# Last block of an S4 convolution: the spectrum's second turn of slots 4 to 7 in two parts, the low half's turn two slots earlier, two sums on GpSimd, one addition on VectorE

## The chip, the cores and the metric

The kernel runs on one core of a Trainium2 chip. The metric is the time of the whole program on the device in microseconds (us); one execution was also taken with the hardware profiler. TensorE (PE in the profile) multiplies matrices, VectorE (DVE), ScalarE (ACT) and GpSimd (POOL) do elementwise work, and SyncE (SP), ScalarE and GpSimd issue DMA transfers from queues of their own. Each engine works through its instructions in program order.

## The reference, cut to what matters

```python
def reference(A_u, A_A_re, ..., B_w1, B_b1, B_w2, B_b2):
    def _A_ref(u, ...):                     # diagonal state space convolution, length L = 2048
        P = jnp.exp(logdA[:, :, None] * l[None, None, :])
        K = jnp.einsum("dn,dnl,dn->dl", Cc, P, dB).real
        Kf, Uf = rfft(pad(K)), rfft(pad(u))
        return irfft(Uf * Kf)[..., :L] + u * Dskip
    def _B_ref(x, w1, b1, w2, b2):
        return gelu(x @ w1 + b1) @ w2 + b2
    x = A_u                                 # (1, 2048, 512)
    xn = _layernorm(x)
    s = _A_ref(xn, ...)
    g = silu(_B_ref(xn, ...))
    return x + s * g
```

Only the convolution `s`, its product with the gate `g` and the addition of `x` bear on the change.

## The kernel before, in words

The first 390 us or so compute the layer norm, the feed-forward gate `g` and the convolution kernels, by a long order written out by hand. The convolution follows, in four blocks of 128 channels (`b` = 0 to 3), each in eight slots (`g` = 0 to 7, function `slot`). The transform of length 4096 is factored into parts of 32 and 64 points. The order of the instructions on every engine is that of the code.

In a slot of the last block TensorE makes the second part of the forward transform of four frequencies (`second_tiles`, L891, tile `s`, in PSUM with two buffers `ri`); ScalarE copies the signal's half (`uh`), VectorE multiplies it with the kernel's spectrum (L910, or L924 in slot 7, two products), and sums and differences of the products give the real and imaginary spectrum `Y` (`combine`, L934 and L936; on GpSimd for slots 0 and 1, else on VectorE). Every two slots make one `Y`; TensorE transforms it back over 64 points (`back_dft`, L945, tiles `sa_p` and `sa_q`), ScalarE copies the result into `Z` (`back_out` L955, `last_out` L963), and VectorE turns `Z` in 32x32 blocks into `T`. `Z` and `T` have a low half, from slots 0 to 3 (turned by `turn`, L989), and a high half, from slots 4 to 7 (turned by `last_turn`, L969).

Slot 7 is done in two columns `jj` with a PSUM tile of their own each (`last_second`, `last_product`), the first of which takes the buffer of slot 5 and the second that of slot 6. Their two columns of `Y` feed the back transform into `sa_q`.

Behind the slots stands the end of the program. `last_half(b, h, i)` is the last transform, over 32 points, of half `h` of the spectrum into output half `i` (L982, `y`): 16 matmuls with 32x32 weights out of `gc` and 256 columns; the results of both `h` add up in PSUM. The profile has two rows for a matmul of float32. An output half has two quarters of the output, `n[0]` and `n[1]`, or `n[2]` and `n[3]`. VectorE multiplies them with the gate: `last_gate_low` (L1040, two products a quarter) for `n[0]` and `n[1]`, `last_gate_high` (L1046, four products) for the rest. `last_add` (L1050) adds `x`: on GpSimd for `n[0]` and `n[1]`, on VectorE for `n[2]` and `n[3]`. `store` issues four transfers a quarter (L1055), on SyncE's and ScalarE's queues in turns, and two of `n[2]` on GpSimd's. The transfers of SyncE and ScalarE go over eight lanes, each with a semaphore; a store that takes a lane waits until the lane's transfer before it has landed.

The low half is turned in two pieces: one in slot 5, `turn(b, 0, 0)`, the other at the end of slot 7, `turn(b, 0, 1)`.

## Time before, and the profile's summary

| | |
|---|---|
| median of 3 runs | 528.2 us (527.54 to 529.6) |
| the profiled execution | 526.64 us |
| its span, first to last instruction | 524.9 us |
| TensorE busy | 507.3 us, 97% of the span |
| VectorE busy | 456.0 us, 87% |
| GpSimd busy | 326.6 us, 62% |
| granted TensorE clock, mean | 0.995 of full speed |

The span is what the rows of the trace cover; the execution's own time is 1.74 us longer. Rows are of one execution. Matmuls overlap, so a busy TensorE is not one at its peak; the last 8 us of the span, behind TensorE's last transforms, belong to the other engines.

### The profile page before, as it was taken

The page shows a single profiled execution, that of the slowest core. Times are in us where ns is not written, and L with a number is a line of the kernel's source. Part 1 is how long each engine was busy: PE and PEld are TensorE (multiplying, and loading weights), DVE is VectorE, ACT ScalarE, POOL GpSimd, SP SyncE. Part 2 cuts the span into 40 slices and gives each one's busy share as a digit, 9 for nine tenths or more (in the row PEclk, how much of TensorE's full clock was granted, in tenths as well). Part 3 has the DMA queues.
Part 4 walks back from the last instruction along what each step waited for, and adds up shares of the span by engine and source line. Part 5 has one row for each costly group of instructions (what it writes and reads, how often), then busy time and mean ns, then how long its engine had stood idle before and what let it go on. Part 6 is the DMA issues. An engine that isn't in the chain of part 4 may idle for free.

```text
span 524.9 us, 13548 instructions
## 1 busy us (share of the span) xinstructions
PE 507.3 (97%) x5439; PEld 372.3 (71%) x5439; DVE 456.0 (87%) x702; ACT 355.8 (68%) x514; POOL 326.6 (62%) x424
## 2 busy tenths in 40 slices
PE   7999999999999999999999999999999999999993
PEld 6777777777777777777777777777844565656671
DVE  6999989997889989999999898799766868597895
ACT  3749976898698789967979997987814333324340
POOL 5647798474848397975874746675236433947632
PEclk9999999999999999999999999999999999999997
DMA  7858875239275939050158467148496969365595
GB/s 202 213 158 232 256 230 161 68 99 307 61 197 168 286 105 338 15 201 31 32 172 214 127 186 196 35 84 165 115 358 220 177 145 144 99 142 101 123 231 132
DMA packets 108527, 85.63 MB, mean 163 GB/s; under 512 B 43436, under 2 KB 84400, under 8 KB 108464
## 3 DMA queue, kind: packets, MB, share of 16 engines
q1 hardware_dynamic: 98208, 65.81, 49.2%
q0 software_dynamic: 8928, 17.96, 11.6%
q10 hardware_dynamic: 1328, 0.98, 0.8%
q8 instruction: 43, 0.70, 0.6%
q14 instruction: 20, 0.16, 0.1%
HBM read 51.18 MB, written 33.55 MB: 161 GB/s over the span
## 4 chain that ended last, share of the span: by engine, by line
PE 66%; DVE 19%; ACT 5%; POOL 3%; issue 3%; POOLq 0%; DVEq 0%; ACTq 0%
PE s L891 10%; PE z L290 7%; PE z L291 7%; PE z L292 7%; PE f L251 6%; PE f L253 6%; PE f L252 6%; PE sa_p L945 6%; PE kg L664 4%; PE s L875 3%; PE ph L602 2%; DVE hl L277 2%; POOL mm L625 2%; DVE e L652 1%; DVE x L354 1%
## 5 line engine op out<-in xcount | busy, mean ns | idle before, releaser
L625 POOL TENSOR_TENSOR mm<-mm,rc 128x32 f32<-128x32 f32 (+4 forms) x150 | 110.0, 734 | 11.8
L290 PE MATMUL z<-w2h,hh 128*128 128x512 f32 x224 | 97.6, 436 | 0.0
L251 PE MATMUL f<-xh,w1h 128*128 128x512 f32 x220 | 90.5, 412 | 0.2 <-DVE xl L386 0.2
L292 PE MATMUL z<-w2h,hl 128*128 128x512 f32 x224 | 88.5, 395 | 0.6 <-DVE hl L277 0.6
L291 PE MATMUL z<-w2l,hh 128*128 128x512 f32 x224 | 88.6, 396 | 0.0
L253 PE MATMUL f<-xh,w1l 128*128 128x512 f32 x220 | 87.0, 395 | 0.0
L252 PE MATMUL f<-xl,w1h 128*128 128x512 f32 x220 | 86.8, 395 | 0.0
L891 PE MATMUL s<-X,mc 128*64 128x256 f32 x512 | 64.4, 393 | 0.6 <-issue 0.5
L910 DVE TENSOR_TENSOR t<-s,uh 128x512 f32<-128x512 f32 x62 | 39.6, 669 | 21.8 <-ACT uh L902 21.6
L622 POOL COPY mm<-rc 128x32 f32<-128x32 f32 x30 | 16.8, 560 | 64.4 <-DVE e L655 42.5
L891 PEld LDWEIGHTS s<-X,mc 128*64 128x64 f32 x512 | 34.2, 135 | 32.0 <-issue 7.6
L648 DVE TENSOR_TENSOR e<-mm,ra 128x1024 f32<-128x1024 f32 x32 | 43.3, 1354 | 14.2 <-ACT ra L636 8.6
L290 PEld LDWEIGHTS z<-w2h,hh 128*128 128x128 f32 x224 | 42.5, 190 | 12.6 <-issue 3.9
L265 ACT ACTIVATE hf<-f,b1s 128x512 f32<-128x512 f32 x56 | 38.1, 687 | 19.3 <-PE f L253 10.1
L902 ACT COPY uh<-s 128x512 f32<-128x512 f32 x31 | 18.2, 586 | 48.3 <-PE s L891 37.5
L292 PEld LDWEIGHTS z<-w2h,hl 128*128 128x128 f32 x224 | 42.1, 188 | 11.0 <-DVE hl L277 1.0
L277 DVE TENSOR_TENSOR hl<-hf,hh 128x512 fp32r<-128x512 f32 x56 | 47.9, 862 | 2.1 <-ACT hh L271 2.0
L253 PEld LDWEIGHTS f<-xh,w1l 128*128 128x128 f32 x220 | 41.3, 188 | 10.2 <-DVE w1l L236 0.3
L251 PEld LDWEIGHTS f<-xh,w1h 128*128 128x128 f32 x220 | 41.5, 189 | 9.9 <-DVE xl L386 0.5
L291 PEld LDWEIGHTS z<-w2l,hh 128*128 128x128 f32 x224 | 42.3, 189 | 8.4
L252 PEld LDWEIGHTS f<-xl,w1h 128*128 128x128 f32 x220 | 41.4, 188 | 9.3
L271 ACT CAST hh<-hf 128x512 fp32r<-128x512 f32 x56 | 34.5, 618 | 19.5 <-PE z L291 19.3
(194 smaller groups left out, 1092.5 us busy)
## 6 DMA issues: line engine op xcount, KB each, us to landing
xs<-x SPq DMA_DIRECT2D x16, 256.0 KB
xt_h<-xh POOLq DMA_DIRECT2D x4, 1024.0 KB, 5.9
xt_l<-xl POOLq DMA_DIRECT2D x4, 1024.0 KB, 7.8
kgd<-ko SPq DMA_DIRECT2D x16, 256.0 KB
za<-zo SPq DMA_DIRECT2D x4, 1024.0 KB
xh<-xt_h POOLq DMA_DIRECT2D x4, 1024.0 KB, 6.6
xl<-xt_l POOLq DMA_DIRECT2D x4, 1024.0 KB, 9.2
zi<-za SPq DMA_DIRECT2D x4, 1024.0 KB
```

The lines of the kernel that those rows point to most:

```text
L251: PE.matmul(p, wh[:, k, :], xh[:, k, :], start=(k == 0), stop=False)
L252: PE.matmul(p, wh[:, k, :], xl[:, k, :], start=False, stop=False)
L253: PE.matmul(p, wl[:, k, :], xh[:, k, :], start=False, stop=(k == KD - 1))
L265: A.activation(hf, pt.pop((v, f)), AF.Gelu_apprx_tanh, bias=b1s[:, f:f + 1])
L277: V.tensor_sub(hl, hf, hh)
L290: PE.matmul(z, hh[:, s], wh, start=(f0 == 0 and not rows), stop=False)
L291: PE.matmul(z, hh[:, s], wl, start=False, stop=False)
L292: PE.matmul(z, hl[:, s], wh, start=False, stop=(f0 == FA - 1))
L625: GP.tensor_mul(mv[:, :, 0:3:2, w:2 * w], mv[:, :, 0:3:2, 0:w], rc[:, 2 + 2 * i:4 + 2 * i, :].rearrange("p j c -> p c j").unsqueeze(3).to_ ...
L648: V.tensor_mul(e1, m1.unsqueeze(1).to_broadcast([P, 2, CH, N1]), ra[:, :, :, :N1])
L891: PE.matmul(p[ka * 64:(ka + 1) * 64, o], SB["mc"][:, 2 * k + jj, o, :], xf[b][:, k, :, :, jj], start=True, stop=True, skip_group_check=True)
L910: V.tensor_mul(sm[b, g // 2][i][:, :, 2 * (g % 2):2 * (g % 2) + 2], p[:, :, i, 1].unsqueeze(1).to_broadcast([P, 2, 2, P]), uh)
```

## The change

The high half's `Z` and `T` get a new shape: slots 4 and 5 (`j` = 0) and slots 6 and 7 (`j` = 1) have blocks of their own. A 32x32 block now holds two time steps, two parts (real, imaginary) and eight frequencies, where it held one step, two parts and sixteen. `last_turn(b, j, ia)` turns `j` = 0 in one instruction of 1024 elements and `j` = 1 in two of 512. The matmuls behind it, `last_quarter(b, j, i)`, read blocks that mix two steps, so `gc` gets four more sets of 32x32 weights, in which the rows of the other step are zero: 32 matmuls of 128 columns for each `j` and `i`, in place of 16 of 256 for both `j`. `gc` grows from 64 to 192 floats a partition (32 KB to 96 KB).

The other piece of the low half's turn goes from slot 7 to slot 5. The two sums of slot 7's first column go to GpSimd. The addition of `n[0]` goes from GpSimd to VectorE. The order of the last matmuls changes with the parts.

```diff
--- before.py
+++ after.py
@@ -129,7 +129,11 @@
     a = 2 * np.pi * n1 * (k1 + 0.25) / N1
     cf = np.tile(np.stack([np.cos(a), -np.sin(a)], 1), (G, 1, 1))
     cg = np.stack([np.cos(a).T, -np.sin(a).T]).reshape(2, 2, N1 // 2, N1)
-    cg = np.tile(cg.transpose(0, 2, 1, 3).reshape(N1, 2 * N1), (G, 1))
+    last = np.zeros((2, 2, N1 // 4, 2, 2, N1))
+    for s in range(2):
+        last[s, :, :, :, s] = cg[:, 1].reshape(2, 2, N1 // 4, N1).transpose(0, 2, 1, 3)
+    cg = np.concatenate([cg.transpose(0, 2, 1, 3).reshape(N1, 2 * N1), last.reshape(N1, 4 * N1)], axis=1)
+    cg = np.tile(cg, (G, 1))
     n2 = np.arange(N2)[:, None]
     k2 = np.arange(N2)[None, :]
     cm = np.zeros((2, 2, N2 // 2, N1, 2, N2))
@@ -795,7 +799,7 @@
         SB["pm"] = pm = opened(p2, "pm", "right")
         SB["ps"] = opened(pz, "psm", "left", bufs=2, space=PSUM)
         SB["tcn"] = pm.tile([P, N1, P], F32, name="tcn")
-        SB["gc"] = pm.tile([P, 2, N1], F32, name="gc")
+        SB["gc"] = pm.tile([P, 6, N1], F32, name="gc")
 
     def table_load(t, src, ks=range(4)):
         w = t.shape[2] if len(t.shape) == 3 else t.shape[2] * t.shape[3]
@@ -923,7 +927,7 @@
         for i in range(2):
             V.tensor_mul(sm[b, g // 2][i][:, :, j], p[:, i, 1].unsqueeze(1).to_broadcast([P, 2, P]), uh[:, jj])
         for c in range(2):
-            combine(b, g // 2, c, V, slice(j, j + 1))
+            combine(b, g // 2, c, V if jj else GP, slice(j, j + 1))
 
     def combine(b, j, c, eng, js=slice(0, 4)):
         t, w = sm[b, j]
@@ -956,31 +960,39 @@
 
     def last_out(b, j, k0, k1, key="p"):
         if (b, "Z", 1) not in yy:
-            yy[b, "Z", 1] = SB["pm"].tile([P, 2, 4, 8, 2, N1 // 2], F32, tag="Z", name=f"Z{b}_1", bufs=2)
+            yy[b, "Z", 1] = SB["pm"].tile([P, 2, 2, 4, 8, 2, N1 // 4], F32, tag="Z", name=f"Z{b}_1", bufs=2)
         for i in range(2):
             for a, p in enumerate(yy[b, j, key]):
-                k = 8 * (j % 2) + 4 * a
-                A.copy(yy[b, "Z", 1][:, i, :, :, :, k + k0:k + k1],
+                A.copy(yy[b, "Z", 1][:, j % 2, i, :, :, :, 4 * a + k0:4 * a + k1],
                        p[:, k0:k1].rearrange("p k (c g i m) -> p i g m c k", c=2, g=4, i=2)[:, i])
 
-    def last_turn(b, i):
+    def last_turn(b, j, ia):
+        if (b, "T", 1) not in yy:
+            yy[b, "T", 1] = SB["pm"].tile([P, 2, 2, 4, 4, N1], F32, tag="T", name=f"T{b}_1", bufs=2)
+        V.transpose(yy[b, "T", 1][:, j, ia].rearrange("p i g m c -> p (i g m c)"),
+                    yy[b, "Z", 1][:, j, ia].rearrange("p i g m c k -> p (i g m c k)"))
+
+    def last_half(b, i):
         if i == 0:
-            yy[b, "T", 1] = SB["pm"].tile([P, 2, 4, 8, N1], F32, tag="T", name=f"T{b}_1", bufs=2)
-        V.transpose(yy[b, "T", 1][:, i].rearrange("p g m c -> p (g m c)"),
-                    yy[b, "Z", 1][:, i].rearrange("p g m c k -> p (g m c k)"))
-
-    def last_half(b, h, i):
-        if h == 0 and i == 0:
             gx[b, "w"] = [SB["ps"].tile([P, 2, TB * P], F32, tag="ri", name=f"y{b}_{r}", bufs=2) for r in range(2)]
             gx[b, 0] = [gx[b, "w"][q // 2][:, q % 2, :256] for q in range(G)]
-        elif h == 0:
+        else:
             gx[b, 1] = [bank(f"y{b}_{q}").rearrange("p e m -> p (e m)")[:, :256] for q in range(G)]
         for g in range(G):
             for q in range(G):
                 r = slice(q * N1, (q + 1) * N1)
-                x = yy[b, "T", 1][r, i, g] if h else yy[b, "T", 0][r, 16 * g + 8 * i:16 * g + 8 * i + 8]
-                PE.matmul(gx[b, i][q][g * N1:(g + 1) * N1], SB["gc"][r, h], x.rearrange("p m c -> p (m c)"),
-                          start=(h == 0), stop=(h == 1), skip_group_check=True)
+                x = yy[b, "T", 0][r, 16 * g + 8 * i:16 * g + 8 * i + 8]
+                PE.matmul(gx[b, i][q][g * N1:(g + 1) * N1], SB["gc"][r, 0], x.rearrange("p m c -> p (m c)"),
+                          start=True, stop=False, skip_group_check=True)
+
+    def last_quarter(b, j, i):
+        for s in range(2):
+            for g in range(G):
+                for q in range(G):
+                    r = slice(q * N1, (q + 1) * N1)
+                    y = gx[b, i][q][g * N1:(g + 1) * N1].rearrange("p (m s c) -> p s m c", s=2, c=N1)[:, s]
+                    PE.matmul(y, SB["gc"][r, 2 + 2 * j + s], yy[b, "T", 1][r, j, i, g],
+                              start=False, stop=(j == 1), skip_group_check=True)
 
     def turn(b, h, i, n=2):
         if i == 0:
@@ -1077,7 +1089,6 @@
             for jj in range(2):
                 last_product(b, g, jj)
             last_out(b, 3, 0, 2)
-            turn(b, 0, 1)
         else:
             spectrum(b, g)
             for x in back:
@@ -1114,6 +1125,7 @@
             turn(b - 1, g // 2, 1)
         if last and g == 5:
             turn(b, 0, 0)
+            turn(b, 0, 1)
         if b and not last and g in (6, 7):
             for q in (0, 1) if g == 6 else (2,):
                 last_gate(b - 1, (q,), GP)
@@ -1193,15 +1205,20 @@
                 slot(b, g)
         b = NB - 1
         back_dft(b, 3, (2, 3), "q")
+        last_turn(b, 0, slice(0, 2))
+        last_half(b, 0)
+        last_quarter(b, 0, 0)
         last_out(b, 3, 2, 4, "q")
         for i in range(2):
-            last_half(b, 0, i)
-            last_turn(b, i)
-            last_half(b, 1, i)
+            last_turn(b, 1, slice(i, i + 1))
+        last_quarter(b, 1, 0)
+        last_half(b, 1)
+        last_quarter(b, 0, 1)
+        last_quarter(b, 1, 1)
         n = [slice(4 * i, 4 * i + 4) for i in range(4)]
         for i in range(2):
             last_gate_low(b, n[i])
-            last_add(b, n[i], GP)
+            last_add(b, n[i], GP if i else V)
         last_gate_high(b)
         for i in range(2, 4):
             last_add(b, n[i])
```

VectorE in slots 5 to 7 of the last block, before (`T_0` is the low half, `t_3_6` the products of slots 6 and 7, `Y_3` their spectrum):

```order
L934 TENSOR_TENSOR Y_2_6420<-t_3_4_6376,t_3_4_6377 128x512
L936 TENSOR_TENSOR Y_2_6420<-t_3_4_6376,t_3_4_6377 128x512
L989 STREAM_TRANSPOSE T_0_6423<-Z_0_6378 128x1024
L910 TENSOR_TENSOR t_3_6_6462<-s_3_6_6433,uh_6_6460 128x2x256
L910 TENSOR_TENSOR t_3_6_6463<-s_3_6_6433,uh_6_6460 128x2x256
L934 TENSOR_TENSOR Y_3_6471<-t_3_6_6462,t_3_6_6463 128x256
L936 TENSOR_TENSOR Y_3_6471<-t_3_6_6462,t_3_6_6463 128x256
```

and now:

```order
L938 TENSOR_TENSOR Y_2_6420<-t_3_4_6376,t_3_4_6377 128x512
L940 TENSOR_TENSOR Y_2_6420<-t_3_4_6376,t_3_4_6377 128x512
L1001 STREAM_TRANSPOSE T_0_6423<-Z_0_6378 128x1024 x2
L914 TENSOR_TENSOR t_3_6_6463<-s_3_6_6434,uh_6_6461 128x2x256
L914 TENSOR_TENSOR t_3_6_6464<-s_3_6_6434,uh_6_6461 128x2x256
L938 TENSOR_TENSOR Y_3_6472<-t_3_6_6463,t_3_6_6464 128x256
L940 TENSOR_TENSOR Y_3_6472<-t_3_6_6463,t_3_6_6464 128x256
```

The second piece of the low half's turn now stands ahead of slot 6's two products.

VectorE from slot 7's first column to the first gate products, before (`T_1` is the high half, `last` the output, `y` the last transform):

```order
L924 TENSOR_TENSOR t_3_6_6462<-s_3_7_0_6474,uh_7_6484 128x2x128
L924 TENSOR_TENSOR t_3_6_6463<-s_3_7_0_6474,uh_7_6484 128x2x128
L934 TENSOR_TENSOR Y_3_6471<-t_3_6_6462,t_3_6_6463 128x128
L936 TENSOR_TENSOR Y_3_6471<-t_3_6_6462,t_3_6_6463 128x128
L924 TENSOR_TENSOR t_3_6_6462<-s_3_7_1_6475,uh_7_6484 128x2x128
L924 TENSOR_TENSOR t_3_6_6463<-s_3_7_1_6475,uh_7_6484 128x2x128
L934 TENSOR_TENSOR Y_3_6471<-t_3_6_6462,t_3_6_6463 128x128
L936 TENSOR_TENSOR Y_3_6471<-t_3_6_6462,t_3_6_6463 128x128
L989 STREAM_TRANSPOSE T_0_6423<-Z_0_6378 128x1024
L969 STREAM_TRANSPOSE T_1_6542<-Z_1_6464 128x1024 x2
L1040 TENSOR_TENSOR last<-y_0_6524,last 128x2x4x32
L1040 TENSOR_TENSOR last<-y_1_6525,last 128x2x4x32
```

and now:

```order
L928 TENSOR_TENSOR t_3_6_6463<-s_3_7_0_6475,uh_7_6485 128x2x128
L928 TENSOR_TENSOR t_3_6_6464<-s_3_7_0_6475,uh_7_6485 128x2x128
L928 TENSOR_TENSOR t_3_6_6463<-s_3_7_1_6476,uh_7_6485 128x2x128
L928 TENSOR_TENSOR t_3_6_6464<-s_3_7_1_6476,uh_7_6485 128x2x128
L938 TENSOR_TENSOR Y_3_6472<-t_3_6_6463,t_3_6_6464 128x128
L940 TENSOR_TENSOR Y_3_6472<-t_3_6_6463,t_3_6_6464 128x128
L972 STREAM_TRANSPOSE T_1_6520<-Z_1_6465 128x1024
L972 STREAM_TRANSPOSE T_1_6520<-Z_1_6465 128x512 x2
L1052 TENSOR_TENSOR last<-y_0_6522,last 128x2x4x32
L1052 TENSOR_TENSOR last<-y_1_6523,last 128x2x4x32
L1062 TENSOR_TENSOR last<-last 128x512
L1052 TENSOR_TENSOR last<-y_0_6522,last 128x2x4x32
```

Two sums (L934, L936) and the turn of `T_0` are gone from between the products and the turns of `T_1`; the first of these turns has kept its size, the second is now two of half the size, and an addition of a quarter stands between the gate products.

ScalarE's stores of the output with the semaphores that they wait for, before (first `n[0]` and `n[1]`, two each, then one of `n[2]` and two of `n[3]`):

```order
L1055 DMA out_dram<-last 32x4x128 [waits DMAHW4_49,DMAHW3_49,Pool_49]
L1055 DMA out_dram<-last 32x4x128 [waits DMAHW6_49]
L1055 DMA out_dram<-last 32x4x128 [waits DMAHW0_49,Pool_49]
L1055 DMA out_dram<-last 32x4x128 [waits DMAHW2_49]
L1055 DMA out_dram<-last 32x4x128 [waits DMAHW3_49,DVE_49]
L1055 DMA out_dram<-last 32x4x128 [waits DMAHW6_49,DVE_49]
L1055 DMA out_dram<-last 32x4x128 [waits DMAHW0_49]
```

and now:

```order
L1067 DMA out_dram<-last 32x4x128 [waits DMAHW4_49,DMAHW3_49,DVE_49]
L1067 DMA out_dram<-last 32x4x128 [waits DMAHW6_49]
L1067 DMA out_dram<-last 32x4x128 [waits DMAHW7_49,Pool_49]
L1067 DMA out_dram<-last 32x4x128 [waits DMAHW2_49]
L1067 DMA out_dram<-last 32x4x128 [waits DMAHW3_49,DMAHW0_49,DVE_49]
L1067 DMA out_dram<-last 32x4x128 [waits DMAHW6_49,DVE_49]
L1067 DMA out_dram<-last 32x4x128 [waits DMAHW0_49]
```

The first pair waits for VectorE's addition in place of GpSimd's, and `n[1]`'s first store has changed its lane with SyncE's (DMAHW7 for DMAHW0). The last store still waits for DMAHW0, which one store of `n[1]` held before and one holds now.

## Rows read from the trace of the kernel before

**Rows 1.** Page, part 4: the chain that ended last, share of the span by engine.

```profile
PE 66%; DVE 19%; ACT 5%; POOL 3%; issue 3%; POOLq 0%; DVEq 0%; ACTq 0%
```

**Rows 2.** End of that chain: start, length (us), engine, names, line.

```profile
515.47 1.07 DVE last L1040 x3
...
517.91 1.10 DVE last L1050
519.29 0.62 POOL out_dram L1055
```

**Rows 3.** VectorE's timeline: start, length, engine, line, operation, shapes, idle before and releaser.

```profile
506.49 1.29 DVE L910 TENSOR_TENSOR t<-s,uh 128x512 f32<-128x512 f32 x2 [0.17 <-ACT uh L902]
...
509.32 0.76 DVE L924 TENSOR_TENSOR t<-s,uh 128x256 f32<-128x256 f32 x2 [0.75 <-ACT uh L922]
...
510.52 0.75 DVE L924 TENSOR_TENSOR t<-s,uh 128x256 f32<-128x256 f32 x2
...
511.71 1.24 DVE L989 STREAM_TRANSPOSE T<-Z 128x1024 f32<-128x1024 f32 x1
512.88 2.36 DVE L969 STREAM_TRANSPOSE T<-Z 128x1024 f32<-128x1024 f32 x2
...
516.47 1.41 DVE L1046 TENSOR_TENSOR last<-y,last 128x256 f32<-128x256 f32 x4
517.91 1.69 DVE L1050 TENSOR_TENSOR last<-last 128x512 f32<-128x512 f32 x2
```

**Rows 4.** Timeline of TensorE and ScalarE, slot 7 and behind it.

```profile
507.70 2.03 PE L891 MATMUL s<-X,mc 128*64 128x256 f32 x16
...
511.65 0.72 PE L945 MATMUL sa_q<-tcn,Y 64*128 64x128 f32 x8 [0.30 <-DVE Y L934]
...
514.17 0.73 PE L982 MATMUL y<-T,gc 32*32 32x256 f32 x32 [0.50 <-DVE T L969]
512.39 0.78 ACT L963 COPY Z<-sa_q 128x128 f32<-128x128 f32 x4 [0.77 <-PE sa_q L945]
```

**Rows 5.** Timeline of the output's engines in short windows; last: durations min/median/max (ns).

```profile
515.16 0.71 DVE L1040 TENSOR_TENSOR last<-y,last 128x256 f32<-128x256 f32 x2
515.96 2.49 POOL L1050 TENSOR_TENSOR last<-last 128x512 f32<-128x512 f32 x2 [12.34 <-DVE last L1040]
518.48 0.38 ACTq L1055 DMA_DIRECT2D out_dram<-last  x1
520.83 0.38 ACTq L1055 DMA_DIRECT2D out_dram<-last  x1
L1050 DVE TENSOR_TENSOR last<-last x2: 680/883/1086, 517.9 to 518.9; 128x512 f32<-128x512 f32 x2
```

**Rows 6.** Groups by line and shape: busy us, mean ns, idle before; GpSimd and VectorE.

```profile
L508 POOL TENSOR_TENSOR pr_wi<-pr_wi,pr_m 128x128 f32<-128x128 f32 x4 | 3.4, 854 | 0.3
L505 POOL TENSOR_TENSOR pr_wr<-pr_wr,pr_m 128x128 f32<-128x128 f32 x4 | 1.9, 464 | 0.3
L883 DVE STREAM_TRANSPOSE X<-s 128x512 f32<-128x512 f32 x64 | 41.2, 686 | 4.7 <-PE s L875 4.7
```

**Rows 7.** Chain rows of small matmuls and first reader of gc; gc's load; page's DMA line.

```profile
378.30 1.93 PE kg L664 x128
441.86 1.03 PE y L1017 x4
L1190 SPq DMA_DIRECT2D gc<-in_cg_dram x1: 328/328/328, 392.5 to 392.5; - x1
DMA packets 108527, 85.63 MB, mean 163 GB/s; under 512 B 43436, under 2 KB 84400, under 8 KB 108464
```

**Rows 8.** Timeline of GpSimd and VectorE around slot 3 and slot 5.

```profile
497.73 5.88 POOL L1034 TENSOR_TENSOR xb<-gb,xb 128x512 f32<-128x512 f32 x4 [2.31 <-DMA xb<-in_A_u_dram]
498.11 1.44 DVE L934 TENSOR_TENSOR Y<-t,t 128x512 f32<-128x512 f32 x1
503.87 0.69 DVE L934 TENSOR_TENSOR Y<-t,t 128x512 f32<-128x512 f32 x1
```

## The prediction

> **What bounds the kernel now.** I read the chain of work that ended last first. Over the whole span two thirds of it is TensorE and a fifth VectorE [rows 1], but every edit that can show lies behind the point where TensorE stops setting the pace: the chain ends with the gate products, the additions and a store [rows 2]. So I took the timeline of that end, one engine after the other. From 509.32 to 519.60 VectorE's rows [rows 3] show no idle time: the turns at L969 (512.88) come straight behind the last turn of the low half (511.71 + 1.24), and ScalarE's first pair of copies, out of the four that start at 512.39, is done by then [rows 4]. The first gate product starts at 515.16 [rows 5], when the second of those turns has left VectorE; the matmuls that it reads (32 rows, 514.17 + 0.73 = 514.90) are done before [rows 4]. Work taken off VectorE between 509 and 515 is therefore worth its time there.
>
> What follows the first gate products is the second thing to see. GpSimd adds the first two quarters of the output one after the other, until 515.96 + 2.49 = 518.45; a store of the second quarter is issued on ScalarE's queue at 518.48, and the last store of all, of the fourth quarter, on the same queue at 520.83 [rows 5]. The fourth quarter itself is ready at 517.91 + 1.69 = 519.60 [rows 3]. By the order of ScalarE's stores the last one waits for a lane, DMAHW0, that the second quarter's store held: 520.83 - 518.48 = 2.35 us. So I read the end of the span as hanging on **when the second quarter is added**, through two stores in a row, and not on the last addition. That is the quantity I forecast.
>
> **The change part by part.** *1. The low half's second turn goes to slot 5.* One turn is 1.24 us and a pair 2.36 [rows 3], so the second adds 1.12 there. VectorE waits 0.17 before slot 6's products (506.49) and 0.75 before slot 7's (509.32) [rows 3]. Slot 6's products start 1.12 - 0.17 = 0.95 late and end at 506.49 + 1.29 + 0.95 = 508.73; the second wait takes 0.75 of that, so slot 7's first products start 0.20 late, at 509.52, and end at 510.28. TensorE meets the lateness once: slot 7's spectrum uses the two buffers of slots 5 and 6, so its second tile, half of the row at 507.70 [rows 4] and so due at about 508.7, must wait for 508.73. That is nothing to 0.30, which is the wait on VectorE in the row at 511.65; I take 0.15, for the restart.
>
> *2. Two sums go to GpSimd.* The first column's products start at 509.32 and take 0.76, the second's start at 510.52 [rows 3]: the sums between them hold VectorE for 0.44. Without them, but with part 1's lateness, the second column's products start at about 510.35, 0.17 earlier, and what follows them starts at 511.54 and not 511.71. GpSimd is idle there. No row shows this sum on GpSimd at 128x128. The nearest are an addition at L505, 464 ns, and a dearer one at L508, 854 ns [rows 6]; those are the ends, and I take 0.52, nearer to the first because less runs beside it in the tail. The handover costs 0.09 (two gate products end at 515.16 + 0.71, GpSimd starts at 515.96 [rows 5]). The sums end at 510.28 + 0.09 + 2 x 0.52 = 511.41. Behind that TensorE has 4 rows of this column and 8 of the other left; 8 took 0.72, from 511.65 to 512.37 [rows 4], 12 take about 0.95: 512.40. ScalarE's copies stay where they were, to 0.05: the first pair is done at 512.87.
>
> *3. The turn in two parts.* The turn of slots 4 and 5 (1.24) stands where the low half's turn stood, from 511.54 to 512.78. Two of half the size follow. A 128x512 turn takes 686 ns in the loop [rows 6], half of the big one would be 620; I take 650. The first needs the copies: 512.9 to 513.55. The first output half needs matmuls behind it: before, 16 matmuls of 256 columns, two rows each (0.73 from the first start to the last end [rows 4]); now 32 of 128, as many columns, while the other 32 run earlier, under the turns. I take 0.73 again. The dear bound is the many small matmuls at L664, 128 rows in 1.93 us or 15 ns a row [rows 7]: 64 rows are 0.96, with the drain 1.2, so 0.5 more. With 0.05 to start, the first gate product begins at 514.33; with the sums held up (below) at 514.58. I take **514.41, 0.75 earlier**.
>
> *4. One addition to VectorE.* The first quarter's addition now stands between the gate products. Undisturbed, one took 680 ns; beside GpSimd 1086 [rows 5]. GpSimd has nothing to do then, so 0.68. The second quarter is added, on GpSimd, by 514.41 + 0.71 for the first two products, 0.03, 0.68, then 0.63 for the next two, 0.09 and 1.26 for GpSimd's addition (half of 2.49 and a little) = 517.81, against 518.45. So the 0.68 costs most of what parts 1 to 3 won on VectorE, and the addition of 1.24 that GpSimd drops ahead of its second gives the rest back. On VectorE the four upper products (1.41 [rows 3]) end about when GpSimd does, and two additions put the fourth quarter at 519.1, half a microsecond before 519.60 and still ahead of its lane.
>
> *5. Larger weights.* The load of the weights, 32 KB before and 96 now, is issued at 392.5 and first read at 441.86 [rows 7]; 49 us hide it. At the mean rate of 163 GB/s [rows 7] the 64 KB would cost 0.4 us without that.
>
> *Sum.* 518.45 - 517.81 = **0.64 us earlier**, carried through two stores of unchanged length to the end. The profiled execution took 526.64, 1.74 more than its span of 524.9, and would take 526.0; the median of the runs shown, 528.2, is 1.56 above that execution, so I forecast **527.6**.
>
> **A lock between two engines.** VectorE's sum at L934 took 1.44 us beside GpSimd's additions (497.73 to 503.61) and 0.69 behind them [rows 8]: an operation of VectorE with both inputs in SBUF is stretched while GpSimd runs. In the changed kernel VectorE's sums of the second column, due at 511.13, meet GpSimd's second sum, which ends at 511.41. If they wait for it, the turn starts 0.28 later and the gate products at 514.58, a gain of 0.47; if they don't, 514.33 and 0.72. The Trainium skill, page SBUF — State Buffer, section "SBUF: two separate sides", calls the port pair of the two engines an exclusive lock, held for the whole instruction, and says that a VectorE operation with two SBUF inputs falls under it; the stretched row agrees in direction, and by this rule it would be the 0.47.
>
> **The rivals.** *Slower: GpSimd's sums become the wait.* At 0.85 each, the dearest row of their size [rows 6], they end at 512.07. VectorE's sums, stretched until then, end at 512.5, TensorE's last rows at 513.1, the turn at 513.75, the first half turn at 514.4, and the first gate product starts at 515.2. The second quarter is added at 518.6, 0.15 after 518.45: 528.4; at 1.0 each it is 0.45 later, 528.7. It decides from about 0.78 a sum. For it: the two sums stand at the head of all that is left. Against: the cheapest row of that size is 0.46. The lock of the page named above is what would hold VectorE back in this case.
>
> *Half-width matmuls cost more.* At 15 ns a row [rows 7] the first gate product starts at 514.9 and the gain shrinks to 0.15: 528.1. For it: twice as many instructions. Against: 32 rows of twice the columns took 0.73 [rows 4], which leaves room for two of the new rows in the time of one.
>
> *More than forecast.* If TensorE isn't held in part 1 and the sums cost 0.46, ScalarE's copies come earlier too; the first product starts at 514.2 and the gain is about 0.9: 527.3.
>
> *The change does nothing for the end.* If the last store doesn't hang on the second quarter's lane, only the half microsecond of the fourth quarter can show: 527.7. Time can't tell this from the forecast; the stores can.
>
> **How the numbers follow.** Chances: the forecast, with the last case that has its time, 0.60; GpSimd's wait 0.15; dearer matmuls 0.12; more gained 0.13. They lie between 527.3 and 528.7. The three runs of before spread over 527.54 to 529.6, and the profiled execution took 526.64, so a median moves by 0.8 or so by itself. I reach 1.4 to either side: 526.2 (the largest gain and that scatter) to 529.0. A change of 0.5% (2.6 us) is about what a measurement of this kernel can tell from none. No case comes near it; faster by more has 0.06 and slower by more 0.04, from scatter alone, and 0.90 is left for within.
>
> **What would show it.** Right: two turns in a row on VectorE ahead of slot 6's products, and these near 507.4; the first gate product near 514.4; GpSimd's one addition of a quarter ending near 517.8; the last store 2.1 to 2.4 us behind one of the second quarter. Wrong: GpSimd's sums at 0.8 us or more with VectorE's sums behind them; a wait of TensorE over 0.3 us in slot 7; the first gate product at 515 or later; a last store that directly follows the fourth quarter's addition; any shift ahead of slot 5, where the program stands as it did.

## The result, and the profile after

| | before | after |
|---|---|---|
| median, us | 527.36 (526.55 to 529.6, 20 runs) | 530.05 (528.3 to 534.19, 20 runs) |
| ratio of after to before, 95% interval | | 1.005 [1.0038, 1.0063] |
| the profiled execution, its span, us | 526.64, 524.9 | 528.3, 526.5 |

The change makes the kernel 0.5% slower, where 0.1% faster was forecast: 2.69 us later in place of 0.64 earlier. (The forecast started from a median of three runs, 528.2; twenty runs give 527.36.) The profiled execution of after is the quickest of its 20; a second one of the same kernel stands with the experiments.

Up to the gate products the trace goes nearly as forecast. The timeline of the changed kernel from slot 6 on (start and us, engine, line, tiles, how many, and in brackets the idle time before and what ended it):

```profile
505.17 2.36 DVE L1001 STREAM_TRANSPOSE T<-Z 128x1024 f32<-128x1024 f32 x2
...
507.46 1.25 DVE L914 TENSOR_TENSOR t<-s,uh 128x512 f32<-128x512 f32 x2
...
507.79 2.19 PE L895 MATMUL s<-X,mc 128*64 128x256 f32 x16
...
509.42 0.75 DVE L928 TENSOR_TENSOR t<-s,uh 128x256 f32<-128x256 f32 x2
...
510.73 0.46 POOL L940 TENSOR_TENSOR Y<-t,t 128x128 f32<-128x128 f32 x1
...
511.21 0.29 DVE L938 TENSOR_TENSOR Y<-t,t 128x128 f32<-128x128 f32 x1
...
511.62 2.46 DVE L972 STREAM_TRANSPOSE T<-Z 128x1024 f32<-128x1024 f32 x3
...
512.91 2.00 PE L994 MATMUL y<-T,gc 32*32 32x128 f32 x125
...
514.96 0.76 DVE L1052 TENSOR_TENSOR last<-y,last 128x256 f32<-128x256 f32 x2 [0.88 <-PE y L994]
...
515.75 0.69 DVE L1062 TENSOR_TENSOR last<-last 128x512 f32<-128x512 f32 x1
...
517.19 1.27 POOL L1062 TENSOR_TENSOR last<-last 128x512 f32<-128x512 f32 x1 [6.00 <-DVE last L1052]
517.29 1.41 PE L994 MATMUL y<-T,gc 32*32 32x128 f32 x87 [0.92 <-issue]
...
518.68 1.42 DVE L1058 TENSOR_TENSOR last<-y,last 128x256 f32<-128x256 f32 x4 [1.58 <-PE y L994]
520.13 1.29 DVE L1062 TENSOR_TENSOR last<-last 128x512 f32<-128x512 f32 x2
521.12 1.16 POOL L1067 DMA_DIRECT2D out_dram<-last  x2 [2.67 <-DVE last L1062]
```

The two turns stand in slot 5 (505.17, x2), slot 6's products start at 507.46 and not at 506.49 [rows 3], and VectorE's sums of the second column are through at 511.62. Three turns follow without a gap. What is new stands at the end: VectorE waits 0.88 us for TensorE before the first gate product (514.96) and 1.58 before the upper output half's products (518.68), and TensorE itself stood still for 0.92 us before its last 87 rows (517.29). Before, the first gate product started at 515.16 [rows 5] and GpSimd's last stores at 519.29 [rows 2]; now at 514.96 and 521.12. So the lower output half comes 0.20 us earlier, and the end 1.83 us later. The quantity that the prediction forecast, the second quarter added on GpSimd at 517.81, is at 517.19 + 1.27 = 518.46 and so as late as before (518.45).

What TensorE waited for is named by the view of its waits between 511 and 520 us (what waited, for what: us in all, times, longest):

```profile
PE y L994 <- issue: 0.9, 1, 0.9
```

The view names no engine, semaphore or transfer that released it: "issue". In the same stretch the granted clock was 1.00, the upper of its two levels, 2.4 GHz, so that is not it either (the columns behind PE are busy us and instructions of the other engines; the last three are the clock, the share of the DMA engines and GB/s):

```profile
511.00:515.00 4.00, 4.00 (x183) 3.25 (x182) 3.09 (x7) 1.57 (x8) 0.19 (x1) 1.00 0.69 200
515.00:520.00 5.00, 2.77 (x160) 2.16 (x156) 3.39 (x9) 0.00 (x0) 1.27 (x1) 1.00 0.41 86
```

And the transfers have a queue that the prediction did not look at, q8, of kind "instruction": the engines' programs are themselves fetched from memory. The page's row of it, of before and then of after:

```profile
q8 instruction: 43, 0.70, 0.6%
```

```profile
q8 instruction: 44, 0.72, 0.6%
```

A packet there is 0.72 MB / 44, some 16 KB. TensorE has 5631 rows of matmul and as many of weight loads in the trace of after, 5439 of each before: 11262 and 10878 instructions. Divided by 256 these are 44.0 and 42.5, and the packets are 44 and 43. My reading is one packet for every 256 instructions of TensorE, or 128 matmul rows. By their own records the packets keep this step through the whole trace of after: from the start of the 11th to that of the 41st TensorE begins 7647 loads and matmuls, 255 a packet. One packet of after starts between 515.0 and 515.2 us, as the view of the transfers shows for that stretch, and the wait ends at 517.29, 2.1 to 2.3 us from the start of the fetch to the first use:

```profile
q8 instruction: 1, 0.02, 30.6%
```

### The profile page after: what moved, and what is told of

Its sections match the earlier page's. It is cut to its first block, busy times and chain, and to the rows that moved or that the text cites. A ratio compares the mean times of both kernels' runs of the same rounds, so it can differ in the third digit from the quotient of the medians.

```text
span 526.5 us, 13936 instructions
## 1 busy us (share of the span) xinstructions
PE 509.7 (97%) x5631; PEld 375.2 (71%) x5631; DVE 456.0 (87%) x702; ACT 355.8 (68%) x514; POOL 326.3 (62%) x425
## 4 chain that ended last, share of the span: by engine, by line
PE 64%; DVE 17%; ACT 5%; DMA 4%; POOL 3%; issue 3%; SPq 0%; POOLq 0%; DVEq 0%; ACTq 0%
PE s L895 10%; PE z L294 6%; PE z L295 6%; PE f L255 6%; PE z L296 6%; PE f L257 6%; PE f L256 6%; PE sa_p L949 6%; PE kg L668 4%; PE s L879 2%; PE ph L606 2%; DMA mc<-in_cm_dram 2%; DMA tcn<-in_ct_dram 2%; DVE hl L281 2%; POOL mm L629 2%
## 5 line engine op out<-in xcount | busy, mean ns | idle before, releaser
L294 PEld LDWEIGHTS z<-w2h,hh 128*128 128x128 f32 x224 | 42.5, 190 | 12.6 <-issue 3.9
```

The lines of the kernel that those rows point to most:

```text
L294: PE.matmul(z, hh[:, s], wh, start=(f0 == 0 and not rows), stop=False)
```

## The experiments

Four theories. **S**: TensorE runs out of instructions in the tail (the rows behind the slots), because padded matmuls use them up faster than blocks of 256 are fetched. **P**: a matmul row of this size costs 15 to 16 ns whatever its columns, so twice as many rows cost twice as much. **C**: columns set the time, as the prediction had it. **M**: the moved turn, sums or addition cost the time.

**1. Three of the four edits, the second turn as before.** Before, with

```diff
-            combine(b, g // 2, c, V, slice(j, j + 1))
+            combine(b, g // 2, c, V if jj else GP, slice(j, j + 1))
...
-            turn(b, 0, 1)
...
+            turn(b, 0, 1)
...
-            last_add(b, n[i], GP)
+            last_add(b, n[i], GP if i else V)
```

> The kernel before with three of the four edits: the low half's turn in slot 5, two sums on GpSimd, one addition on VectorE. The second turn and its 16 matmuls of 256 columns stay as before. Theory S (TensorE runs out of instructions in the tail, because the zero-padded weights make 192 more rows of matmuls there) and theory P (a row of 128 columns costs TensorE as much as one of 256, so the tail is longer by the count): not slower than before, 0.996 to 1.001, and no wait of TensorE marked issue behind 512 us. Theory M (the moved turn, sums and addition cost the time): slower by 1 us or more, 1.003 to 1.006, with VectorE's or GpSimd's rows late.

Measured: 527.8 us against 527.19, ratio 1.001 [0.9996, 1.0025]. No wait marked issue in the tail; TensorE's 96 rows of 256 columns run through in one piece, 24 ns a row, and the addition now delays the upper products:

```profile
513.04 2.37 DVE L969 STREAM_TRANSPOSE T<-Z 128x1024 f32<-128x1024 f32 x2 [1.07 <-ACT Z L963]
...
514.34 2.30 PE L982 MATMUL y<-T,gc 32*32 32x256 f32 x96 [1.14 <-DVE T L969]
...
517.36 1.40 DVE L1046 TENSOR_TENSOR last<-y,last 128x256 f32<-128x256 f32 x4
...
519.78 1.17 POOL L1055 DMA_DIRECT2D out_dram<-last  x2 [1.00 <-DVE last L1050]
```

M falls for the loss of 0.5%. The turn waits 1.07 us for ScalarE's copies: what the sums won on VectorE is lost there again.

**2. Only the turn in two parts with padded weights.** The changed kernel's `gc`, `last_out`, `last_turn`, `last_half`, `last_quarter` and their order; turn, sums and addition as before. Against the changed kernel:

```diff
-            combine(b, g // 2, c, V if jj else GP, slice(j, j + 1))
+            combine(b, g // 2, c, V, slice(j, j + 1))
...
+            turn(b, 0, 1)
...
-            turn(b, 0, 1)
...
-            last_add(b, n[i], GP if i else V)
+            last_add(b, n[i], GP)
```

> The change's second turn in two parts with the zero-padded weights alone; the low half's turn, the two sums and the addition stay where they were before. S and P: slower than before by 2 to 4 us, 1.004 to 1.008, with the upper gate products waiting 1 us or more for TensorE. S also says a wait of 0.8 us or more marked issue in TensorE's last rows; P says no such wait is needed. M: within 0.5 us of before.

Measured: 530.25 us, ratio 1.0054 [1.0035, 1.0073]. This edit alone gives the whole loss, within the noise. TensorE's rows show the same wait, again with 87 rows behind it:

```profile
515.71 1.85 PE L994 MATMUL y<-T,gc 32*32 32x128 f32 x125 [0.46 <-DVE T L972]
...
520.22 1.41 PE L994 MATMUL y<-T,gc 32*32 32x128 f32 x87 [1.21 <-issue]
```

**3. The changed kernel again, unchanged.**

> The changed kernel once more, for a second profile: its 20 runs had a median of 530.05 where the profiled one took 528.3. S: this profile, if its time is near 530, shows the wait marked issue in TensorE's tail longer than 0.92 us or a second one, by the difference of 1 to 2 us. P and M: TensorE's tail has the same rows and waits, and the difference lies elsewhere.

Measured: 531.0 us, ratio 1.0067 [1.0047, 1.0087]. Its profiled execution (span 528.6) has two waits, the first 32 + 75 rows into the tail's 320, that is with 213 behind it, the second with 87, so 126 rows apart (128 are 256 instructions; a few instructions are no matmuls):

```profile
513.85 1.30 PE L994 MATMUL y<-T,gc 32*32 32x128 f32 x75
515.79 0.92 PE L994 MATMUL y<-T,gc 32*32 32x128 f32 x50 [0.64 <-issue]
...
519.37 1.41 PE L994 MATMUL y<-T,gc 32*32 32x128 f32 x87 [1.20 <-issue]
```

From the row of slot 7's spectrum to the end of the span the first trace of after takes 526.5 - 507.79 = 18.7 us, this one 528.6 - 508.73 = 19.9, and before 524.9 - 507.70 [rows 4] = 17.2. The last two are 2.7 us apart, as the medians are. Of the 2.11 us between the two executions of after (530.41 and 528.3), 0.94 stands ahead of this row, where the second trace has TensorE wait 0.76 us for VectorE at 54.27, and 1.2 in the tail, 0.92 of it more wait. So the second wait is a part of why the median lies above the profiled 528.3, and not the most of it.

**4. Sixteen small matmuls in an early wait** of the changed kernel (32 rows, 64 instructions); they feed nothing.

```diff
+    def small(n):
+        p = ps1.tile([P, P], F32, tag="f1", name="small", bufs=2)
+        for _ in range(n):
+            PE.matmul(p[:N1, :N1], ident[:N1, :N1], ident[:N1, :N1], start=True, stop=True, skip_group_check=True)
...
+        small(16)
```

> The changed kernel with 16 small matmuls (32 rows of matmuls and 32 of weights) more in the prologue, where TensorE waits for the layer norm; nothing else changes. S: instructions come in blocks, and 64 more at the start move the place in the tail at which the block ends by 64 rows; the wait marked issue (0.92 us at 517.29 in the changed kernel) moves to an earlier row or changes its length by 0.3 us or more, and the time with it, by 0.3 to 1.5 us either way. P and M: same time as the changed kernel within 0.3 us.

Measured: 531.62 us, ratio 1.0073 [1.0046, 1.0101]; the time is not clear of the changed kernel's 1.0067 in experiment 3. The test is the place of the wait, which has moved from 87 to 119 rows before the end; 119 - 87 is the 32 that were added some 400 us earlier:

```profile
516.34 1.85 PE L1000 MATMUL y<-T,gc 32*32 32x128 f32 x125
...
520.47 1.82 PE L1000 MATMUL y<-T,gc 32*32 32x128 f32 x119 [1.24 <-issue]
```

The view of TensorE's waits over the whole span says more: a burst of `kg` rows in the early part ran dry too, where before has no such wait.

```profile
PE kg L673 <- issue: 1.6, 1, 1.6
```

**5. 32 columns in place of 128** in each padded matmul: three quarters of those products are left out.

```diff
-                    y = gx[b, i][q][g * N1:(g + 1) * N1].rearrange("p (m s c) -> p s m c", s=2, c=N1)[:, s]
-                    PE.matmul(y, SB["gc"][r, 2 + 2 * j + s], yy[b, "T", 1][r, j, i, g],
+                    y = gx[b, i][q][g * N1:(g + 1) * N1].rearrange("p (m s c) -> p s m c", s=2, c=N1)[:, s, :1]
+                    PE.matmul(y, SB["gc"][r, 2 + 2 * j + s], yy[b, "T", 1][r, j, i, g, :1],
```

> The changed kernel whose zero-padded matmuls read 32 columns in place of 128 (three of four steps of slots 4 to 7's share are left out of the sum); as many rows of matmuls as before. Theory P (a row costs TensorE some 15 ns whatever its columns): the first 125 of these rows still take 1.8 to 2.0 us, and the time is that of the changed kernel within 1 us. Theory C (columns set the time): they take 1.0 us or less. S: the wait marked issue still stands 87 rows of matmuls before the end.

Measured: 529.79 us, ratio 1.0044 [1.0026, 1.0061], as slow as with 128. The first 75 rows take 0.91 us and not 1.30, but the waits grow to 1.28 and 1.29 us from 0.64 and 1.20 (experiment 3), at the same rows:

```profile
512.45 0.91 PE L994 MATMUL y<-T,gc 32*32 32x32 f32 x75
514.64 0.66 PE L994 MATMUL y<-T,gc 32*32 32x32 f32 x53 [1.28 <-issue]
...
517.95 1.13 PE L994 MATMUL y<-T,gc 32*32 32x32 f32 x87 [1.29 <-issue]
```

C falls for the kernel's time, and so does P in its plain form: the columns do set a part of a row's price (0.91 / 75 = 12 ns, against 17), but quicker rows only reach the end of the block sooner.

**6. 256 columns in place of 128,** the opposite.

```diff
-                    y = gx[b, i][q][g * N1:(g + 1) * N1].rearrange("p (m s c) -> p s m c", s=2, c=N1)[:, s]
-                    PE.matmul(y, SB["gc"][r, 2 + 2 * j + s], yy[b, "T", 1][r, j, i, g],
+                    y = gx[b, i][q][g * N1:(g + 1) * N1].rearrange("p (m c) -> p m c", c=N1)
+                    PE.matmul(y, SB["gc"][r, 2 + 2 * j + s], yy[b, "T", 1][r, j, i, g // 2 * 2:g // 2 * 2 + 2].rearrange("p g m c -> p (g m) c"),
```

> The changed kernel, with each of the 256 matmuls on padded weights made to read and write 256 columns in place of 128 (the output is then not the reference's: each such product is added to both of its column sets). As many rows and instructions, twice the columns. Rows of 256 columns took 24 ns each in the run with the whole turn (96 in 2.30 us), so 128 of them would take about 3.0 us instead of the 1.85 to 2.0 of the changed kernel. Theory S (TensorE runs out of instructions): instructions are then used more slowly, so the waits marked issue shrink, from 0.6 to 1.3 us to 0.6 us or less each, at the same counts (215 and 87 rows from the end), and part of the longer rows is paid with the shorter waits: ratio 1.004 to 1.008. If the waits came from anything but the rate at which rows are used, they stay at 0.9 to 1.3 us, and the two longer bursts come on top, about 2 us in all: ratio 1.008 to 1.011. Theory C (columns set the time): the 1.1 us a burst is added, with no word on the waits.

Measured: 531.1 us, ratio 1.0065 [1.0051, 1.0079]. The waits shrink to 0.28 and 0.70 us, at the same rows, and the kernel is as slow as with 128 columns (1.005, and 1.0067 in experiment 3):

```profile
513.69 1.94 PE L994 MATMUL y<-T,gc 32*32 32x256 f32 x75
515.91 1.18 PE L994 MATMUL y<-T,gc 32*32 32x256 f32 x44 [0.28 <-issue]
...
519.50 2.04 PE L994 MATMUL y<-T,gc 32*32 32x256 f32 x87 [0.70 <-issue]
```

With 32, 128 and 256 columns a stretch of 75 rows takes 0.91, 1.30 and 1.94 us and the wait behind it 1.28, 0.64 and 0.28: the sums are 2.19, 1.94 and 2.22. That is S: what comes next is there about 2 us after the burst began, whatever TensorE does meanwhile.

**7. Without the matmuls of the odd steps:** half of the padded products are left out, 128 rows fewer.

```diff
-        for s in range(2):
+        for s in range(1):
```

> The changed kernel without every second zero-padded matmul (those of the odd steps are left out of the sum): 64 rows fewer for each output half, 128 in all, which is one block of 256 instructions. S: the block's end that fell 87 rows before the end of the program lies behind it now, so the 1.2 us wait is gone; P: the first 64 rows take about 1.0 us, and the first gate product starts 0.8 to 1.0 us earlier. Both: 0.997 to 1.000 of before; M (if the moved parts cost): still slower by 1 us or more.

Measured: 527.1 us, ratio 0.9995 [0.9978, 1.0012]. A wait of 0.47 us is left. That it has 87 rows behind it is chance: the program has 5503 rows now, and 5503 - 87 = 5416 is, counted from the start, the place of the wait that had 213 of 5631 behind it in experiment 3 (5418). The first gate product comes at 514.22, 0.74 earlier than in after:

```profile
514.22 0.76 DVE L1052 TENSOR_TENSOR last<-y,last 128x256 f32<-128x256 f32 x2
...
515.28 0.48 PE L985 MATMUL y<-T,gc 32*32 32x256 f32 x12 [0.47 <-issue]
...
515.74 4.83 ACTq L1067 DMA_DIRECT2D out_dram<-last  x7
516.45 1.27 POOL L1062 TENSOR_TENSOR last<-last 128x512 f32<-128x512 f32 x1 [5.25 <-DVE last L1052]
...
516.88 1.42 DVE L1058 TENSOR_TENSOR last<-y,last 128x256 f32<-128x256 f32 x4 [0.51 <-PE y L994]
...
519.33 1.16 POOL L1067 DMA_DIRECT2D out_dram<-last  x2 [1.61 <-DVE last L1062]
```

With 192 rows in the tail, still 64 more than before, the edits together win nothing. The trace shows why, and against the prediction: GpSimd has added the second quarter at 516.45 + 1.27 = 517.72, 0.73 us earlier than the 518.45 of before, ScalarE's queue is through at 515.74 + 4.83 = 520.57, ahead of the start of its last store before (520.83 [rows 5]), and the span is 524.8 against 524.9. VectorE still waits 0.51 us for TensorE before the upper products, and GpSimd's stores of the third quarter start at 519.33, against 519.29 [rows 2]. The span ends 4.2 to 4.5 us behind their last issue here, in before and in after; what ends it is taken up below.

**8 and 9. Thirty-two and 48 small matmuls,** in two early waits of the changed kernel (of 9 the diff; 8 has 16 in each).

```diff
+        small(24)
...
+        small(24)
```

> The changed kernel, with 16 small 32 x 32 matmuls in each of two waits of the early part, 32 in all, that is 64 instructions (a load and a matmul each) more than the run with 16. Theory S: a wait stands where 256 instructions are used up, 64 rows earlier in the tail than in the changed kernel, so with 87 + 64 = 151 and 215 + 64 = 279 rows behind it, and one could stand 23 rows from the end. If waits hung on a place in the code (the first padded row after a turn, say) they would stay with 87 and 215 rows behind them. The time is not compared: the bursts of the early part (128 rows of 15 ns) can run dry as well, as the two runs with small matmuls have shown, so 529 to 536 us.

> The changed kernel with 48 small matmuls (192 instructions) more in the prologue's two waits of TensorE. S: the ends of blocks move by 96 rows: waits marked issue stand at 183 or 311 rows before the end, or 55, and none at 87 or 215. P: no wait moves. The prologue itself may be up to 1 us longer, so the waits and their places are the test, not the time.

Measured: 532.91 us, ratio 1.0099 [1.0085, 1.0114], and 537.72 us, ratio 1.0189 [1.0168, 1.0211]. With 32 the waits are 0.97 us with 12 + 9 + 11 + 96 + 23 = 151 rows behind it, and 1.90 with 23; the one at 279 did not show. With 48 they are 1.44 us behind the first 32 + 107 of the tail's 320 rows, that is with 181 to go (183 were expected), and 2.11 with 55; the view of the waits adds two in `kg`:

```profile
517.62 0.48 PE L992 MATMUL y<-T,gc 32*32 32x256 f32 x12 [0.97 <-issue]
...
518.02 1.70 PE L1001 MATMUL y<-T,gc 32*32 32x128 f32 x96
521.62 0.48 PE L1001 MATMUL y<-T,gc 32*32 32x128 f32 x23 [1.90 <-issue]
```

```profile
520.05 1.72 PE L1001 MATMUL y<-T,gc 32*32 32x128 f32 x107
523.21 0.46 PE L1001 MATMUL y<-T,gc 32*32 32x128 f32 x19 [1.44 <-issue]
...
527.60 0.99 PE L1001 MATMUL y<-T,gc 32*32 32x128 f32 x55 [2.11 <-issue]
```

```profile
PE kg L673 <- issue: 3.8, 2, 2.6
PE y L1001 <- issue: 3.5, 2, 2.1
```

The place follows the count of instructions from the start of the program, over four counts: with no small matmuls and with 16, 32 and 48, the waits stand behind 5418, 5544, 5546 or 5672 rows of the program, 126 to 128 apart. The trace with 48 is 536.4 - 526.5 = 9.9 us longer than after's first: 3.8 of it are the two dry bursts of `kg`, 2.6 more wait in the tail, and 2.0 the matmuls themselves, which are longer than the waits they were put into (the matmuls behind them, L265, start at 15.97 and not at 14.01). Where the rest went I did not follow up.

**10. Padded weights for the lower output half only**; the upper half with one turn of 1024 and 16 matmuls of 256 columns as before, the other edits kept (224 rows in the tail, 96 fewer than in the changed kernel). The core of the diff against the changed kernel:

```diff
-        for i in range(2):
-            last_turn(b, 1, slice(i, i + 1))
+        last_turn(b, 1, 0)
+        last_turn(b, 1, 1)
...
-        last_quarter(b, 0, 1)
-        last_quarter(b, 1, 1)
+        last_half(b, 1, 1)
```

> A version that might beat both: the zero-padded parts for the first output half alone, the second half with one turn of 1024 and 16 matmuls of 256 columns as before, and the other three edits; 224 rows of matmuls behind the slots in place of 320 (before: 128). S and P: no wait marked issue of 0.8 us or more at the end, the upper gate products no longer wait for TensorE, time 0.998 to 1.001 of before. If a wait stays, up to 1.004.

Measured: 529.0 us, ratio 1.0023 [1.0011, 1.0035]: better than the change, not than before. One wait is left, 0.72 us, in the middle of the padded burst; its place, behind 32 + 75 of 224 rows, is 213 - 96 = 117 rows from the end:

```profile
513.99 1.48 PE L1001 MATMUL y<-T,gc 32*32 32x128 f32 x75
516.18 0.92 PE L1001 MATMUL y<-T,gc 32*32 32x128 f32 x50 [0.72 <-issue]
```

**11. Two of the four edits:** the turn in slot 5 and the sums (experiment 1 without the addition). Against experiment 1:

```diff
-            last_add(b, n[i], GP if i else V)
+            last_add(b, n[i], GP)
```

> The kernel before, with two of the edits only: the low half's second turn in slot 5 and two sums on GpSimd; the second turn as before and both additions on GpSimd. Beside the run with three edits (ratio 1.001) it prices the moved addition alone. Theories S and P say nothing of a loss here: ratio 0.998 to 1.002. Theory M: 1.003 or more if the sums or the turn cost. The step of the prediction on the addition (0.68 on VectorE, its result earlier than by GpSimd's 1.27) expects the same as with three edits or up to 0.6 us more.

Measured: 527.39 us against 527.73, ratio 0.9995 [0.9986, 1.0004]. The moved turn and sums change nothing, at either sign: the high half's turn starts at 512.85 after a wait of 1.07 us for ScalarE's copies, where before it started at 512.88 [rows 3].

```profile
512.85 2.37 DVE L969 STREAM_TRANSPOSE T<-Z 128x1024 f32<-128x1024 f32 x2 [1.07 <-ACT Z L963]
...
519.28 1.17 POOL L1055 DMA_DIRECT2D out_dram<-last  x2 [0.84 <-DVE last L1050]
```

With the addition GpSimd's stores start at 519.78 (experiment 1) and without it at 519.28. No version beat the kernel before.

## Why the prediction was wrong

**The step that failed is step 3**, "now 32 of 128, as many columns" and "I take 0.73 again". Two groups of 64 rows stood behind the first turn, and their 125 recorded rows took 2.00 us, 16 ns each. That is the dear bound of the same step, from `kg` (1.93 us for 128 [rows 7]); the first gate product came at 514.96 and not at 514.41. The bound had 0.5 us for it, the trace 0.55. I set it aside for the wrong comparison: 32 rows of twice the columns in 0.73 us include the drain of the last, and show no room for two rows in the time of one (24 ns for a row of 256 columns, twice 16 for two of 128).

**What no step had is the supply of instructions.** The tail's rows rose from 128 to 320, so its blocks from one to two and a half, used up in about 2 us each. The step priced one output half and stopped where VectorE took over; the upper half's 160 rows were never priced. In the first trace of after 0.92 of the 1.83 us at the end is the wait; I put the other 0.9 to the rows themselves. With 128 rows fewer (experiment 7) GpSimd's stores start 1.79 earlier, at 519.33, 0.45 of it from the shorter wait. In the second trace the waits are 1.84 us. That the number of rows and instructions, and not that of columns, sets the time is shown by experiments 2, 5, 6 and 7, that the place is a count by 3, 4, 8, 9 and 10.

That the waits are for instruction packets rests on these counts, on the number of packets and on their times; no view names the packet as the releaser. By the packets' own records all 15 waits marked issue in the tails of these traces, and the three in `kg`, end 2.2 to 3.0 us behind the start of a packet on q8 and 1.2 to 1.5 us behind its end. In the second trace of after the packets start at 513.36 and 516.89, and the waits end at 515.79 and 519.37. This also tells why the wait 213 rows from the end is missing in the first trace of after: its packet started at 511.74, 1.17 us ahead of the first padded row (512.91), in the second trace only 0.49 ahead (513.85). What sets the start of a packet stays open.

**The end was read only in part**, in "the end of the span as hanging on when the second quarter is added". For before that path is there: the second quarter's store lands at 520.81, the last store starts at 520.83 and lands at 523.52, and SyncE, which waits for it, is through at 524.10. But GpSimd's last long instruction, a DRAIN of 4.17 us that starts beside its last store, ends at 523.93. That second path hangs on VectorE's addition of the third quarter [rows 2] and is only 0.17 us shorter. The view of SyncE's waits from 515 to 526 us in the trace of before, and then GpSimd's DRAINs in before and in after (ns min/median/max, first and last start):

```profile
SPq L1236 <- DMA out_dram<-last: 2.5, 2, 1.7
```

```profile
L1236 POOLq DRAIN  x3: 46/98/4171, 519.8 to 524.6; - x3
```

```profile
L1253 POOLq DRAIN  x3: 46/103/4140, 521.6 to 526.2; - x3
```

In after GpSimd's DRAIN ends last, at 525.73, against SyncE's 525.39. In experiment 7 the second quarter is added 0.73 us earlier than before and the last store lands at 523.16, 0.36 earlier; SyncE is through at 523.73, but GpSimd at 524.03, because the third quarter is no earlier, and the span is 0.1 shorter. So what is won on the second quarter shows only as far as the third keeps up, and the upper half's rows held that back. On the forecast's own times, with the upper quarters half a microsecond earlier, the second path would have cost next to nothing. The rival "does nothing for the end" had the path of before wrong; its sign to look for, a last store behind the fourth quarter's addition, is what after shows.

**The rest by its steps.** *1*: slot 6's products started 0.97 late (0.95 forecast; 0.09 of the 0.97 is from further up); slot 7's at 509.42 (509.52). TensorE was held there about as forecast (0.15): the row at 507.79 is 2.19 us and not 2.03 [rows 4], though the profile names no wait on VectorE. *2*: 0.46 a sum (0.52), the nearest row's price [rows 6]; done at 511.19. The rival that GpSimd's sums become the wait falls. VectorE's sums start at 511.21, 0.02 later, so the two did not meet and the lock was not tested. (The time for that case has a slip: 511.54 + 0.28 + 1.24 + 0.65 + 0.73 + 0.05 is 514.49, not 514.58; no bound hangs on it.) *4*: the addition took 0.69 (0.68), and cost nothing in after only because VectorE waits 1.58 us behind it anyway; where it does not wait, the stores come 0.5 later (experiment 1 against 11). The second quarter's 0.65 of lateness against 517.81 is 0.55 from the first gate product and 0.1 from the terms behind it; that the four upper products end about when GpSimd does failed with the upper half's rows. *5*: no wait on the load of `gc` shows in the tail. The rival of the half-width matmuls (528.1, chance 0.12) had the first gate product right, 514.9, and missed the upper half as the forecast did.

The Trainium skill, page TensorEngine Tiling (Array Packing), section "Instruction Overhead", gives each matmul an overhead of about 60 cycles, so that one column takes as long as 60, and advises against splitting a dimension that is already small. The traces agree that there is a price beside the columns: a row takes 24 to 26 ns with 256 columns, 15 to 17 with 128 and 12 with 32. By the page's figure, 25 ns at 2.4 GHz as an estimate, a row would cost more than the 12 to 17 ns measured; two rows, one matmul of the program, took 24 with 32 columns, and which of the two the figure is for no run here shows.

## What to carry to other kernels

Count instructions before columns when a matmul is split: here the dear row of the trace, 15 ns for a small matmul, was the right price, and 192 more rows cost more than all that VectorE won. Price every burst that the change makes longer, and not only the one ahead of the first wait. In a burst of small matmuls look for waits marked "issue" and at the instruction queue: their place follows the number of instructions from the start of the program, so that an edit far ahead can move such a wait into another burst. And where two paths end within 0.2 us of each other, as the stores of ScalarE and GpSimd do here, what is won on one shows only up to the other: follow the one that the chain of the profile names as well as your own reading.

## What was not expected of the hardware

- TensorE's instructions come in packets of some 16 KB, by the counts one for 256 of them, and in bursts at 12 to 26 ns a matmul row TensorE stands still for 0.28 to 2.11 us at places 126 to 128 rows apart, until 1.2 to 1.5 us behind the end of a packet. The burst of 96 rows of 256 columns, at 24 ns (before and experiments 1 and 11), shows no such wait.
- Adding 16, 32 and 48 matmuls of 32x32 in the early part, where they took 1.19, 2.38 and 3.40 us, moved the waits of the tail some 400 us later by 32, 64 and 96 rows, to within 2. The ratios were 1.0073, 1.0099 and 1.0189, against 1.005 for the changed kernel in its first runs and 1.0067 in experiment 3.
- For 75 rows, a stretch of rows and the wait behind it took 1.94 to 2.22 us together, from 32 to 256 columns.
- GpSimd's DRAIN, 4.14 to 4.24 us from about its last store on, ended the work in after and in experiment 7, 0.3 us behind SyncE's wait for the last store.
